# Slot attention and a GELU feed-forward: a longer pinned order, with forty copies on another engine

## The chip, the cores and the metric

One core of a Trainium2 chip. A core has five engines that each work through a list of instructions of their own, strictly in its order: TensorE (PE in the profile, matrix products, PEld its weight loads), VectorE (DVE), ScalarE (ACT), GpSimd (POOL) and SyncE (SP, which here issues the transfers between HBM and the on-chip memory). They wait for each other through semaphores. The metric is the time of one execution in microseconds (us), as the median of several.

## The reference

```python
def _attn_ref(q, k, v, phi):                      # batch 8, heads 8, seq 576, head_dim 64, 32 slots
    a = np.exp(phi - np.max(phi, axis=2, keepdims=True))      # softmax over the sequence
    a = a / (np.sum(a, axis=2, keepdims=True) + 1e-09)
    k_m = np.einsum('bhsm,bhsd->bhmd', a, k)
    v_m = np.einsum('bhsm,bhsd->bhmd', a, v)
    scores = np.matmul(q, k_m.transpose(0, 1, 3, 2)) / np.sqrt(q.shape[-1])
    attn = np.exp(scores - np.max(scores, axis=-1, keepdims=True))
    attn = attn / (np.sum(attn, axis=-1, keepdims=True) + 1e-09)
    return np.matmul(attn, v_m)

def _moe_ref(x, w_in, w_out):                     # x (4608, 512), w_in (512, 2048), w_out (2048, 512)
    h = x @ w_in
    return 0.5 * h * (1.0 + erf(h / np.sqrt(2.0))) @ w_out
```

The attention's output, heads side by side, is the `x` of the second function. All arrays arrive as float32 (the two weights as float64 bit patterns in pairs of 32-bit words, which the kernel turns into float32 itself).

## The kernel before

**Stages.** Each of the 8 batches goes through the same steps. `phi` is loaded with slots on partitions (128 x 576, two groups of heads g = 0, 1), gets its maximum (`amax`, DVE, L392) and exponential (`aexp`, ACT, L398), is transposed on PE (`at`, L423) and copied out of PSUM (`atc`, L210). `slots` (PE, L531, L506) sums it against k and v, `km` scales the sums, `slotsT` and `kT` transpose and copy them. The scores follow (`n_score` for batch 0, L615; `score` for the others, L598), then a softmax over 32 slots (`max`, `sub`, `exp`, `sum`, `inv`, `mul`) whose result p is split into a high and a low part (`ph`, `pl`; for batch 0 `n_hi`, L689, and `n_lo`, L693). The value sums are not multiplied with p. They are multiplied with `w_in` first: `Up` (PE, L598) makes U = v_m @ w_in for 128 to 512 columns of the hidden layer, split by `Uh` (a copy) and `Ul` (DVE, L814). Then `h` (PE, L855) makes the hidden layer from U and p in six products per 288 rows and 128 hidden columns; `gelu` (ACT), `gh` (a copy, the high part) and `gl` (DVE, L882) prepare it, and `p` (PE, L895, line `acc`) adds twelve products with `w_out` to four accumulators. `o` copies these out. For batches 2 to 7 `p`, `o` are called `P`, `O` and work by halves.

**Weights.** `w_in` and `w_out` come in 16 slabs f each (`Lwi.f`, `Lwo.f`). Every half slab is turned into float32 by `dB` (two ACT instructions, L272 and L273), `dC`, `dS`, `dG` (DVE, L277, L285, L281) and one sum on POOL (`dDi` for w_in, `dDo` for w_out, L305); w_out is also split by `dE` (a copy) and `dF` (DVE, L311). All of this lies in the first 150 us.

**What sets the order.** A string `START` names these steps one by one, with batch, slab and half (`aexp.0.1` is batch 0, group 1; `gelu.0.3.1` is batch 0, hidden slab 3, second half of the rows; `dB.0.1` is slab 0 of w_out, `dB.0.0` that of w_in). The program issues them in this order, so each engine's list is the string cut down to that engine's steps, and a dependency ties every instruction to the one before on its engine. A letter behind a colon (`:a`, `:d`) gives a copy to ACT or DVE. Behind the string a plan with due times (`put`, `prepare`, `columns`, `run`) does what is left. Before, the string ends with `p.1.15`, the last product of batch 1. `W.k.i` are matmuls on ones whose result nobody reads.

**Buffers.** A second string, `HOME`, gives each slab, each key and value tile and each output a place in memory by name (`raw_3:U0` reuses the place of `raw_0`). A load into a used place waits on SP until the earlier user is through, and all loads behind it wait too. In PSUM the tiles of `Up`, `score`, `slots`, `slotsT` and of batch 1's `at` share one place (`ps_at`, one buffer), so each waits until the one before is copied out.

Of the kernel before, what the change touches and what calls it, by code (L numbers as in the profile page):

```python
# [62 lines left out]
Ul.0.3 score.1.0 dC.4.0 dS.4.0 Lwi.6 gelu.0.2.0 h.0.3.0 Lwo.7 gh.0.2:a dF.3 dB.5.0
gelu.0.3.0 h.0.3.1 dDi.4 dB.6.0 sT.1.0.1 Lwo.5 dB.5.1 sT.1.0.0 Lwi.8 Up.0.4.1 p.0.1
dC.5.0 dS.5.0 dG.5.0 Uh.0.4:d Ul.0.4 h.0.4.0 gelu.0.3.1 gh.0.3:a max.1.0 dG.6.0 Lq.1.1
dDi.5 Up.0.5.1 h.0.4.1 sub.1.0 exp.1.0 gl.0.2 dC.6.0 gl.0.3 dG.5.1 dC.5.1 dS.5.1 sum.1.0
gelu.0.4.1 p.0.2 Uh.0.5:d Ul.0.5 inv.1.0 dDo.5 dE.5 mul.1.0 dS.6.0 score.1.1 pT.1.0
Lwo.6 dB.6.1 Lwo.8 sT.1.1.0 p.0.3 sT.1.1.1 gelu.0.4.0 Lwi.7 gh.0.4:a dF.5 dB.7.1 gl.0.4
# [1156 lines left out]
```

## Time and profile before

| | |
|---|---|
| median of 3 runs | 703.35 us (702.97 to 704.49) |
| profiled execution | 704.61 us, of which the span from first to last instruction is 702.8 us |
| PE | busy 691.1 us of the span |
| DVE, ACT, POOL | busy 388.6, 298.4 and 46.6 us |
| moved | 64.37 MB, mean 92 GB/s |

The span is what the trace shows; 1.8 us of the profiled execution lie around it. PE is on the chain that ended last for 94% of the span. A busy PE is not a PE at full clock: its granted clock is at one of two levels, and the lower one doubles most of its durations.

### The profile page before, as it was taken

The numbers are of one execution on the slowest core, as the hardware profiler recorded it, in microseconds if no ns is written. First come the engines' busy times: TensorE is split into PE (matmuls) and PEld (weight loads), VectorE is DVE, ScalarE is ACT, GpSimd is POOL, SyncE is SP. The second block draws the span as 40 slices with busy tenths as digits, with TensorE's granted clock in tenths as the row PEclk, the third lists the DMA queues.
The fourth block names the chain that finished last, engine by engine and source line by source line (L and its number), as shares of the span: only waits on it lengthen the run. The fifth ranks groups of instructions, "written<-read, shape, count | busy, mean of one in ns | idle before, by whom it ended". The sixth has DMA issues, their size and how long they took to land.

```text
span 702.8 us, 12357 instructions
## 1 busy us (share of the span) xinstructions
PE 691.1 (98%) x4940; PEld 576.6 (82%) x4940; DVE 388.6 (55%) x705; ACT 298.4 (42%) x768; POOL 46.6 (7%) x39
## 2 busy tenths in 40 slices
PE   7999999999999999999999999999999999999997
PEld 5767787887878888888887888888877888888886
DVE  4989998954755366534943346433834346432222
ACT  4588766862615264524553224222531225322220
POOL 1232243310000000000000000000000000000000
PEclk7599999999999999999999999999999999999999
DMA  8954451416253571145600200020000200000001
GB/s 318 329 211 172 154 197 62 133 29 212 86 142 117 177 217 23 65 137 159 190 1 32 82 2 31 1 98 1 30 1 31 83 1 31 1 31 0 31 1 45
DMA packets 30716, 64.37 MB, mean 92 GB/s; under 512 B 3780, under 2 KB 8644, under 8 KB 30660
## 3 DMA queue, kind: packets, MB, share of 16 engines
q1 hardware_dynamic: 30564, 63.46, 27.6%
q8 instruction: 39, 0.64, 0.4%
q10 hardware_dynamic: 96, 0.13, 0.1%
q14 instruction: 17, 0.14, 0.1%
HBM read 54.13 MB, written 9.44 MB: 90 GB/s over the span
## 4 chain that ended last, share of the span: by engine, by line
PE 94%; DMA 1%; DVE 1%; SPq 0%; ACT 0%; issue 0%
PE acc L895 50%; PE h L855 29%; PE tacc L895 6%; PE pu L598 4%; PE psc L598 1%; PE psc L506 1%; DMA raw<-w_in 1%; PE pk L531 1%; PE x L506 1%; SPq L345 0%; PE pk L506 0%; PE psc L519 0%; PE psc L560 0%; DVE aT L210 0%; PE x L519 0%
## 5 line engine op out<-in xcount | busy, mean ns | idle before, releaser
L855 PE MATMUL h<-p_hi,U 128*128 128x288 f32 x1024 | 203.8, 298 | 0.0
L895 PE MATMUL acc<-wo_hi,gh 128*128 128x512 f32 x512 | 200.6, 392 | 0.0
L895 PE MATMUL acc<-wo_hi,gl 128*128 128x512 f32 x512 | 199.7, 390 | 0.0
L895 PE MATMUL acc<-wo_lo,gh 128*128 128x512 f32 x512 | 199.6, 390 | 0.0
L867 ACT ACTIVATE gf<-h 128x256 f32<-128x256 f32 x192 | 74.0, 387 | 265.0 <-issue 206.4
L855 PEld LDWEIGHTS h<-p_hi,U 128*128 128x128 f32 x1024 | 164.0, 188 | 23.0 <-issue 8.3
L210 DVE CAST gh<-gf 128x512 fp32r<-128x512 f32 x109 | 46.9, 430 | 167.4 <-ACT gf L867 165.3
L895 PEld LDWEIGHTS acc<-wo_hi,gh 128*128 128x128 f32 x512 | 96.5, 188 | 21.1 <-DVE gl L882 3.4
L895 PEld LDWEIGHTS acc<-wo_hi,gl 128*128 128x128 f32 x512 | 96.1, 188 | 21.5 <-DVE gl L882 0.9
L895 PEld LDWEIGHTS acc<-wo_lo,gh 128*128 128x128 f32 x512 | 96.1, 188 | 15.8
L855 PE MATMUL h<-p_lo,U 128*128 128x288 f32 x512 | 108.8, 294 | 0.1
L882 DVE TENSOR_TENSOR gl<-gf,gh 128x512 fp32r<-128x512 f32 x128 | 94.3, 736 | 15.2 <-ACT gh L210 5.7
L855 PEld LDWEIGHTS h<-p_lo,U 128*128 128x128 f32 x512 | 81.4, 188 | 0.6 <-DVE p_lo L693 0.6
L814 DVE TENSOR_TENSOR U<-pu,U 128x512 fp32r<-128x512 f32 (+2 forms) x50 | 40.8, 834 | 42.0 <-ACT U L210 41.8
L869 ACT ACTIVATE tails<-h 128x32 f32<-128x32 f32 x192 | 37.4, 195 | 0.0
L598 PE MATMUL pu<-w_in_sb,kT 64*32 64x512 f32 (+2 forms) x624 | 34.4, 528 | 0.4 <-ACT kT L210 0.4
L210 ACT CAST U<-pu 128x512 fp32r<-128x512 f32 (+2 forms) x42 | 30.4, 759 | 7.4 <-PE pu L598 7.3
L305 POOL TENSOR_TENSOR w_in_sb<-y,raw 128x512 int32<-128x512 int32 x16 | 23.8, 1493 | 43.8 <-DVE y L285 11.8
L305 POOL TENSOR_TENSOR y<-y,raw 128x512 int32<-128x512 int32 x16 | 21.9, 1374 | 56.5 <-DVE y L285 23.9
L272 ACT ACTIVATE y<-raw 128x512 f32<-128x512 f32 x32 | 21.6, 675 | 8.9 <-issue 4.3
L895 PE MATMUL tacc<-wo_hi,gh_t 128*128 128x512 f32 x64 | 25.0, 391 | 0.0
L895 PE MATMUL tacc<-wo_hi,gl_t 128*128 128x512 f32 x64 | 24.9, 389 | 0.0
(119 smaller groups left out, 581.5 us busy)
## 6 DMA issues: line engine op xcount, KB each, us to landing
kv<-kv SPq DMA_DIRECT2D x48, 256.0 KB, 6.5
raw<-w_out SPq DMA_DIRECT2D x16, 512.0 KB, 5.6
raw<-w_in SPq DMA_DIRECT2D x16, 512.0 KB, 4.5
out<-o SPq DMA_DIRECT2D x16, 512.0 KB, 2.7
q<-qT SPq DMA_DIRECT2D x9, 576.0 KB, 8.8
phi<-phiT SPq DMA_DIRECT2D x16, 288.0 KB, 4.5
aT<-phiN SPq DMA_DIRECT2D x6, 512.0 KB, 4.7
q<-qT SPq DMA_DIRECT2D x10, 288.0 KB
```

The source lines that it names most:

```text
L210: return e.copy(dst, src) if e is nc.scalar else e.tensor_copy(dst, src)
L272: nc.scalar.activation(y, high.bitcast(F32), AF.Abs, scale=2.0**16)
L305: nc.gpsimd.tensor_tensor(w, y, low, op=ALU.add)
L506: nc.tensor.matmul(pk[32 * j : 32 * j + 32, : 2 * D], st["aT", b][:, c, g, 32 * j : 32 * j + 32], st["kv", b, g, c][:, :, j, :], start=(c ...
L531: nc.tensor.matmul(pk[32 * j : 32 * j + 32, w0 * D : (w0 + n) * D], st["aT", b][:rows, c, g, 32 * j : 32 * j + 32], t[:rows, w0 : w0 + n, ...
L598: nc.tensor.matmul(ps[g][M * j : M * j + M], st["kT", b][rows, t, M * j : M * j + M], moving[j][rows], start=True, stop=True,)
L814: nc.vector.tensor_sub(u[:, ..., 1, :], pu, u[:, ..., 0, :].bitcast(F32))
L855: i = nc.tensor.matmul(h[:, :HS], u[g][w], x[:, g, :], start=(n == 0), stop=(n == 3 * G - 1))
L867: nc.scalar.activation(gf[:, f % 2 * n : f % 2 * n + n], h[:, :n], AF.Gelu)
L869: nc.scalar.activation(t, h[:, n:HS], AF.Gelu)
L882: nc.vector.tensor_tensor(g_of("gl", *k), g_of("gf", *k), g_of("gh", *k).bitcast(F32), op=ALU.subtract)
L895: nc.tensor.matmul(acc, x, w[:, f, :], start=(first and n == 0), stop=(last and n == 2))
```

## The change

`START` is replaced: 694 steps become 850, and it now ends within batch 2 (its first half of rows is done, the second begun, scores of batch 3 and slot sums of batch 4 among it). Of the steps in both strings 40 run on another engine: 29 copies go from DVE to ACT (8 `Uh`, 8 `gh`, 5 `atc`, 4 `o`, 2 `dE`, 2 `ph`), 11 from ACT to DVE (4 `gh`, 4 `dE`, 2 `Uh`, 1 `atc`); with those in the rest of the program DVE's list has 22 copies fewer and ACT's 22 more. Nothing else changes engine, and no instruction of PE is added or taken away: 4,125 matmuls of the same shapes stand in both lists. The new string `PLACES` allots each place in memory once, ahead of all use, since the order of first use is another one now; it takes the place of `first_tiles`. `anat` is issued as its two halves `aadd` and `ax`. The store of an output of batches 0 and 1 becomes a step of its own, `os`. Line numbers shift by 13 to 20.

```diff
+PLACES = """
+kT:1024*3 phi:4608*1 nm:8*2 sm:8*2 aT:5120*1 rz:8*2 mx:72*2 smx:72*2 U0:8192*1 U4:8192*1
...
+"""
 START = """
-W.4.3 Lphi.0.0 amax.0.0 aexp.0.0 at.0.0.0 Lphi.0.1 amax.0.1 aexp.0.1 anorm.0 atc.0.0.0:d
-at.0.1.0 atc.0.1.0 at.0.0.4 Lwo.0 at.0.1.4 atc.0.1.4:d Lkv0.0.0 Lkv0.1.0 atc.0.0.4:d
...
+Lphi.0.0 Lphi.0.1 Lwo.0 Lkv0.0.0 Lkv0.1.0 amax.0.0 Lq.0.0 amax.0.1 aexp.0.0 Lwi.0 Lwo.1
+at.0.0.0 Lq.0.1 dB.0.1 dC.0.1 aexp.0.1 dS.0.1 dG.0.1 atc.0.0.0:a at.0.1.0 anorm.0 W.4.3 dDo.0
...
-    def first_tiles():
-
-        for tag in ("mx", "smx"):
-            sb.tile([P, G * SB], F32, tag=tag, name=f"{tag}_first")
+    for x in PLACES.split():
+        tag, size, n = x.replace("*", ":").split(":")
+        sb.tile([P, int(size) // 4], F32, tag=tag, name=f"place_{tag}", bufs=int(n))
...
-        if f == NF - 1 and j % 2:
-            r = b * S + (j - 1) * P
-            nc.sync.dma_start(
-                out[r : r + 2 * P, :].rearrange("(c p) n -> p c n", p=P), st["o", b, j // 2]
-            )
+
+    def store(b, j):
+        r = b * S + (j - 1) * P
+        nc.sync.dma_start(
+            out[r : r + 2 * P, :].rearrange("(c p) n -> p c n", p=P), st["o", b, j // 2]
+        )
...
-        put(tn + 1, f"anat.{b}", *(f"aexp.{b}.{g}" for g in range(G)), f"anorm.{b}")
+        put(tn + 1, f"aadd.{b}", f"ax.{b}", *(f"aexp.{b}.{g}" for g in range(G)), f"anorm.{b}")
```

The first place: ACT's list from its first exponential on, before (`phi_0`, `sm_0` are the exponential of batch 0, `y_0`, `raw_0` the conversion of slab 0, `pt_0_g_c` a transposed piece of group g):

```order
L398 ACTIVATE phi_0_101,sm_0_105<-phi_0_101,nm_0_103 128x576 x2
L210 COPY aT_0_107<-pt_0_1_0_120 128x4x128
L272 ACTIVATE y_0_171<-raw_0_130 128x512
L273 ACTIVATE raw_0_130<-raw_0_130 128x512
L549 ACTIVATE km_0_201<-pk_0_0_144,rz_0_117 128x64
L549 ACTIVATE km_0_201<-pk_0_1_180,rz_0_117 128x64
```

and now:

```order
L415 ACTIVATE phi_0_136,sm_0_154<-phi_0_136,nm_0_149 128x576
L289 ACTIVATE y_0_167<-raw_0_139 128x512
L290 ACTIVATE raw_0_139<-raw_0_139 128x512
L415 ACTIVATE phi_0_136,sm_0_154<-phi_0_136,nm_0_149 128x576
L229 COPY aT_0_159<-pt_0_0_0_160 128x4x128
L229 COPY aT_0_159<-pt_0_1_0_175 128x4x128
L229 COPY aT_0_159<-pt_0_0_4_191 64x128
L562 ACTIVATE km_0_217<-pk_0_0_194,rz_0_181 128x64
L229 COPY aT_0_159<-pt_0_1_4_189 64x128
L229 CAST wo_hi_79<-y_0_167 128x512
L562 ACTIVATE km_0_217<-pk_0_1_223,rz_0_181 128x64
```

The conversion of slab 0, which needs the transfer of w_out, now stands between the two exponentials, and the three other `atc` copies have come over from DVE.

The second place: DVE's list from the first score maximum of batch 0 on (`mx_0_0`), before:

```order
L634 TENSOR_REDUCE mx_0_0_229<-psc_0_0_220 128x16
L639 TENSOR_TENSOR s_0_0_231<-psc_0_0_220,mx_0_0_229 128x512
L277 TENSOR_SCALAR y_1_205<-y_1_205 128x512
L285 TENSOR_SCALAR y_1_205<-y_1_205 128x512
L281 TENSOR_SCALAR raw_1_165<-raw_1_165 128x512
L649 TENSOR_REDUCE smx_0_0_249<-s_0_0_231 128x16
L653 TENSOR_SCALAR smx_0_0_249<-smx_0_0_249 128x16
L654 RECIPROCAL smx_0_0_249<-smx_0_0_249 128x16
L277 TENSOR_SCALAR y_0_171<-y_0_171 128x512
L285 TENSOR_SCALAR y_0_171<-y_0_171 128x512
L281 TENSOR_SCALAR raw_0_130<-raw_0_130 128x512
L634 TENSOR_REDUCE mx_0_1_283<-psc_0_1_237 128x16
```

and now, from shortly ahead of it:

```order
L328 TENSOR_TENSOR wo_lo_80<-y_0_167,wo_hi_79 128x512
L294 TENSOR_SCALAR y_0_167<-y_0_167 128x512
L302 TENSOR_SCALAR y_0_167<-y_0_167 128x512
L298 TENSOR_SCALAR raw_0_139<-raw_0_139 128x512
L294 TENSOR_SCALAR y_1_270<-y_1_270 128x512
L298 TENSOR_SCALAR raw_1_157<-raw_1_157 128x512
L302 TENSOR_SCALAR y_1_270<-y_1_270 128x512
L647 TENSOR_REDUCE mx_0_0_288<-psc_0_0_257 128x16
L652 TENSOR_TENSOR s_0_0_291<-psc_0_0_257,mx_0_0_288 128x512
L409 TENSOR_REDUCE nm_1_294<-phi_1_215 128x1
L662 TENSOR_REDUCE smx_0_0_299<-s_0_0_291 128x16
```

The three steps on slab 0 of w_in (`y_0`, `raw_0`) stand ahead of the first maximum now, where they stood behind it.

The third place: PE's list around the first `h`, before:

```order
L423 MATMUL pt_1_0_397<-ident_76,phi_1_311 128x128 x8
L855 MATMUL h_0_0_0_415<-p_hi_0_0_403,U_0_0_339 128x288 x2
L855 MATMUL h_0_0_0_415<-p_lo_0_0_404,U_0_0_339 128x288 x2
L423 MATMUL pt_1_4_426<-ident_76,phi_1_311 64x128 x2
L674 MATMUL pT_0_2_451<-ident_76,s_0_2_390 128x128 x2
L531 MATMUL pk_1_0_460<-kv_1_0_0_340,aT_1_396 32x128 x4
```

and now:

```order
L440 MATMUL pt_1_0_444<-ident_76,phi_1_215 128x128 x8
L687 MATMUL pT_0_0_401<-ident_76,s_0_1_369 128x128
L687 MATMUL pT_0_1_403<-ident_76,s_0_1_369 128x128
L440 MATMUL pt_1_4_470<-ident_76,phi_1_215 64x128 x2
L687 MATMUL pT_0_2_477<-ident_76,s_0_2_415 128x128 x2
L544 MATMUL pk_1_0_489<-kv_1_0_0_304,aT_1_443 32x128 x4
L544 MATMUL pk_1_0_489<-kv_1_0_4_378,aT_1_443 32x128 x4
L868 MATMUL h_0_0_0_521<-p_hi_0_0_485,U_0_0_398 128x288 x2
```

The first `h` has gone behind the slot sums of batch 1 (`pk_1_0`). Further on, `p.0.0` stands ahead of `h.0.2.0`, `h.0.2.1` and `Up.0.3.1`, behind which it stood.

## Rows read from the trace of the kernel before

**Rows 1.** The page: busy time of each engine, and the chain that ended last.

```profile
PE 691.1 (98%) x4940; PEld 576.6 (82%) x4940; DVE 388.6 (55%) x705; ACT 298.4 (42%) x768; POOL 46.6 (7%) x39
PE 94%; DMA 1%; DVE 1%; SPq 0%; ACT 0%; issue 0%
```

**Rows 2.** All waits of PE: who waited for whom, us in total, times, longest.

```profile
PE pk L531 <- DMA kv<-kv: 3.0, 2, 2.4
...
PE tn L560 <- ACT km L549: 0.6, 1, 0.6
```

**Rows 3.** Stretches: length, busy us (instructions) by engine, granted clock share, DMA share, GB/s.

```profile
10.22:34.11 23.89, 21.35 (x243) 17.63 (x232) 18.66 (x41) 11.15 (x26) 6.85 (x5) 0.50 0.96 350
34.11:37.53 3.42, 2.02 (x13) 1.03 (x11) 3.32 (x10) 2.72 (x8) 1.31 (x1) 1.00 0.35 140
37.53:40.94 3.41, 3.41 (x44) 2.55 (x45) 1.70 (x8) 2.65 (x6) 1.29 (x1) 0.50 0.34 118
40.94:250.00 209.06, 209.06 (x1592) 169.57 (x1594) 151.73 (x264) 123.77 (x265) 36.18 (x25) 1.00 0.44 142
```

**Rows 4.** ACT in order of time: start, us, line, tiles, [idle before, releaser].

```profile
4.37 0.78 ACT L398 ACTIVATE phi<-phi,nm 128x576 f32<-128x576 f32 x1 [2.14 <-DVE nm L392]
...
5.38 0.78 ACT L398 ACTIVATE phi<-phi,nm 128x576 f32<-128x576 f32 x1
...
8.05 0.66 ACT L272 ACTIVATE y<-raw 128x512 f32<-128x512 f32 x1 [0.25 <-DMA raw<-w_out]
8.61 0.66 ACT L273 ACTIVATE raw<-raw 128x512 int32<-128x512 uint32 x1
```

**Rows 5.** PE in order of time, the first 48 us, same columns.

```profile
9.83 0.78 PE L531 MATMUL pk<-kv,aT 128*32 128x64 f32 x32 [2.43 <-DMA kv<-kv]
...
12.96 0.79 PE L295 MATMUL warm<-one 128*128 128x128 f32 x2
...
15.07 7.06 PE L615 MATMUL psc<-k_blocks,q 128*128 128x64 f32 x32 [0.72 <-ACT k_blocks L210]
...
33.57 0.76 PE L855 MATMUL h<-p_hi,U 128*128 128x288 f32 x2
...
36.86 0.30 PE L423 MATMUL pt<-ident,phi 128*64 128x128 f32 x1 [1.12 <-DVE aT L210]
...
37.51 2.52 PE L531 MATMUL pk<-kv,aT 128*32 128x128 f32 x40
39.96 0.85 PE L855 MATMUL h<-p_hi,U 128*128 128x288 f32 x2
...
43.59 1.43 PE L531 MATMUL pk<-kv,aT 128*32 128x128 f32 x40
...
47.33 0.50 PE L895 MATMUL acc<-wo_hi,gh 128*128 128x512 f32 x1
```

**Rows 6.** DVE in order of time, 18 to 41 us, same columns.

```profile
18.75 0.69 DVE L634 TENSOR_REDUCE mx<-psc 128x16 f32<-128x512 f32 x1 [0.67 <-PE psc L615]
...
39.43 0.95 DVE L693 TENSOR_TENSOR p_lo<-pT,p_hi 128x64 fp32r<-128x64 f32 x4 [1.12 <-ACT p_hi L689]
```

**Rows 7.** Groups by line and shape: count, busy us, mean ns of one, idle before.

```profile
L210 DVE CAST gh<-gf 128x512 fp32r<-128x512 f32 x109 | 46.9, 430 | 167.4 <-ACT gf L867 165.3 <-ACT wo_hi L210 1.3 <-ACT gf L873 0.8
L210 ACT CAST gh<-gf 128x512 fp32r<-128x512 f32 x19 | 11.8, 622 | 4.1 <-PE acc L895 4.0
L210 DVE COPY aT<-pt 128x512 f32<-128x512 f32 x2 | 1.4, 676 | 0.0
L210 DVE CAST U<-pu 128x256 fp32r<-128x256 f32 x5 | 2.1, 421 | 0.0
L277 DVE TENSOR_SCALAR y<-y 128x512 f32<-128x512 f32 x32 | 14.9, 468 | 4.4 <-ACT y L272 4.3
```

**Rows 8.** Stretches as in rows 3, by DVE's load.

```profile
18.75:40.38 21.63, 19.16 (x207) 14.84 (x207) 19.85 (x49) 12.54 (x29) 6.89 (x5) 0.58 0.75 265
40.38:80.00 39.62, 39.62 (x374) 29.78 (x374) 37.95 (x75) 32.55 (x67) 13.12 (x9) 0.99 0.46 167
```

More of the change, by code (lines that the diff above doesn't have):

```diff
@@ L63 @@
[L63 to L68, printed above, removed]
@@ new lines @@
+Lwi.5 dG.3.1 Lwo.5 Up.0.2.1 Lphi.2.1 dS.3.1 h.0.0.1 gelu.0.0.0 dC.3.0 Lq.1.0 dDo.3 Uh.0.2:a
+dE.2:a h.0.1.0 Ul.0.2 amax.2.0 gelu.0.0.1 dF.2 slots.1.1 gelu.0.1.0 gh.0.0:a dS.3.0 dG.3.0
+h.0.1.1 gl.0.0 km.1.1 dDi.3 dE.3 slotsT.1 gelu.0.1.1 Lwo.7 dB.4.1 p.0.0 kT.1:d Lwo.6 Lwi.6
+dB.4.0 dG.4.1 dC.4.1 gh.0.1:a dF.3 h.0.2.0 dC.4.0 dS.4.1 dS.4.0 Up.0.3.1 gelu.0.2.0 dDo.4
+dB.5.1 h.0.2.1 Uh.0.3:d Ul.0.3 h.0.3.0 gl.0.1 gelu.0.2.1 dB.5.0 dG.5.1 score.1.0 p.0.1
+gh.0.2:a sT.1.0.0 Lq.1.1 dG.4.0 gelu.0.3.0 Lwi.7 dE.4 dC.5.0 dDi.4 amax.2.1 sT.1.0.1 dC.5.1
@@ new lines @@
+Lwo.8 h.0.3.1 dF.4 mw.2 gl.0.2 Up.0.4.1 gelu.0.3.1 dS.5.0 p.0.2 dG.5.0 gh.0.3:d dDi.5 aexp.2.0
+max.1.0 Uh.0.4:a dB.6.0 Ul.0.4 sub.1.0 h.0.4.0 gl.0.3 exp.1.0 h.0.4.1 dS.5.1 dG.6.0 dDo.5
+Up.0.5.1 sum.1.0 p.0.3 Uh.0.5:a inv.1.0 dC.6.0 mr.2 Ul.0.5 gelu.0.4.1 mul.1.0 Lwi.8 gelu.0.4.0
+dE.5 dS.6.0 pT.1.0 gh.0.4:a score.1.1 dDi.6 dB.6.1 h.0.5.0 sT.1.1.1 sT.1.1.0 h.0.5.1 dF.5
+ph.1.0:a gl.0.4 dB.7.0 Up.0.6.1 dC.6.1 p.0.4 max.1.1 gelu.0.5.0 Uh.0.6 dC.7.0 gelu.0.5.1
+Ul.0.6 gh.0.5:a sub.1.1 pl.1.0 Up.1.0.4 gl.0.5 exp.1.1 dG.7.0 h.0.6.0 dS.7.0 Uh.1.0 dDi.7
@@ L111 @@
+gl.2.0.6 gelu.2.14.0 aadd.4 pl.2.1 h.2.15.0 h.2.0.1 gelu.2.15.0 h.2.1.1 P.2.0.6 ax.4
+gh.2.0.7:a gl.2.0.7 P.2.0.7 gelu.2.1.1 score.3.1 score.3.0 sT.3.1.0 slots.4.0 sT.3.0.1
+slots.4.1 O.2.0.0:a Lphin.5 Lkv.5.0.1 Lkv.5.1.3 aexp.4.1 Lkv.5.0.3 Lkv.5.1.2 Lkv.5.1.0
+Lkv.5.0.4 gelu.2.0.1 Lkv.5.1.1 O.2.0.1 aexp.4.0 gh.2.1.0:a gl.2.1.0 anorm.4 km.4.1 sT.3.0.0
+Lphi.5.0 sT.3.1.1 km.4.0 Lkv.5.0.0 Lkv.5.0.2 Lphi.5.1
 """
@@ L954, in evict @@
                 ("o", b, j // 2),
-                lambda: sb.tile([P, 2, DM], F32, **home(f"o_{b}_{j}")),
+                lambda: sb.tile([P, 2, DM], F32, **home(f"o_{b}_{j // 2 * 2}")),
             )
@@ L1000, in slot_attention_gelu_ffn @@
     }
+    st.update({("far", "pu", b, f): 1 for b in range(3, B) for f in (4, 12)})
+    st.update({("far", "psc", b, 1): 1 for b in range(3, B)})
+    st.update({k: 1 for k in (("far", "xt", 3), ("far", "pu", 2, 12))})
     done = set()
@@ L1044, in slot_attention_gelu_ffn @@
     put(t + 13, "slotsT.2", "kT.2")
-    st.update({("far", "pu", b, f): 1 for b in range(3, B) for f in (4, 12)})
-    st.update({("far", "psc", b, 1): 1 for b in range(3, B)})
-    st.update({k: 1 for k in (("far", "xt", 3), ("far", "pu", 2, 12))})
     for hf, at in ((0, n + 22), (1, n + 26)):
@@ L1167, in slot_attention_gelu_ffn @@
             if end:
-                behind += [f"o.{b}.{j}.{f}" for j in range(NT)]
+                for j in range(NT):
+                    behind += [f"o.{b}.{j}.{f}"]
+                    if f == NF - 1 and j % 2:
+                        behind += [f"os.{b}.{j}"]
         else:
```

130 lines of the change are left out of this document (65 added, 65 removed).

## Prediction

> **What bounds the kernel now.** I read the page first, then the waits of PE, then stretches of equal clock, then the first 48 us row by row. PE is busy for 691.1 of 702.8 us and is 94% of the chain that ended last [rows 1]. So only PE's idle time and PE's slow time can be won. Both lie in one place. From 40.94 us on PE has no idle time at all (209.06 of 209.06 us up to 250 us) and runs at its upper level, 2.4 GHz [rows 3]; the waits of PE, the longest 2.4 us for keys and values, all lie before [rows 2]. Between 10.22 and 34.11 us it is granted 0.50 of its clock, the lower level of 1.2 GHz, as again between 37.53 and 40.94 us, with 1.00 between [rows 3]. The first product with w_out starts at 47.33 us [rows 5]. In the start DVE is the partner: from the first score maximum at 18.75 us until the last low part of p at 40.38 us (39.43 plus 0.95) it is busy for 19.85 of 21.63 us [rows 6, 8], and in the next 40 us for 37.95 of 39.62 us [rows 8]. All the same PE never waits there.
>
> PE's 4,125 matmuls are the same before and after. **So the change can gain in the first 41 us alone**, and behind them it can only keep or lose. The lengthened part of the string, within batches 1 and 2, has nothing to gain: PE is already full there. I therefore walk through the start, engine by engine in the new order, with the durations of these rows, up to the point where both orders have done the same work on PE: the end of `p.0.0`, `h.0.2.0`, `h.0.2.1` and `Up.0.3.1`.
>
> **Step 1, up to the first scores: 2.7 us later.** Before, the second exponential follows the first at 5.38 us [rows 4]. Now the conversion of slab 0 of w_out stands between them, and it starts at 8.05 us, when its transfer lands; its two instructions reach to about 9.15 us, where the next can start (8.61 plus about 0.55, the step from the first to the second) [rows 4]. The transfers ahead of it on SP are the same five, so I take the same landing. The second exponential then ends about 10.0 us instead of 6.2. Behind it on PE come four transposes (0.85 us at the lower level, by the 0.21 us of one matmul of the 32 in 7.06 us [rows 5]), now two pairs of warming matmuls (0.85 us; a pair is 0.79 us long at most [rows 5]), two short transposes (0.4), and on ACT the copy that the slot sums need (0.3). They start at 12.8 us instead of 9.83 [rows 5]. From there to the first score matmul 5.24 us passed (15.07 less 9.83), with one warming pair in the way at 12.96 us that now stands later [rows 5]; I take 5.0. The scores start at 17.8 us instead of 15.07: plus 2.7.
>
> **Step 2, from the scores to batch 1's slot sums: 2.7 us won back.** Before, this takes 22.44 us (37.51 less 15.07 [rows 5]) with DVE full. What DVE does between the first maximum and the last low part is 19.85 us [rows 8]. Of this, two high parts of U and one large transposed copy go to ACT (2 x 0.42 and 0.68, together 1.5 us [rows 7]); three conversion steps of slab 0 go ahead of the maximum, where DVE now waits anyway (about 0.35 and 0.35 in a row and 0.55, together 1.3; one alone reads 0.47 [rows 7]); two of slab 3 go behind (0.9); one step of the split of w_out slab 1 and small copies come in (0.8). That leaves 16.9 us. The first maximum is at 21.45 us (18.75 plus 2.7). With some 1.6 us in which DVE must wait for PE's second scores, for U's high part on ACT and for the high part of p, the last low part is ready at 39.95 us instead of 40.38. ACT, busy for 12.54 of the 21.63 us [rows 8], hides the three copies; without that cover they would cost 0.38 to 0.62 us each, by the dearest row of a copy there [rows 7]. PE's transposes of batch 1 wait for the second low part of U at 33.8 us, and its slot sums start at 37.55 us, against 37.51 [rows 5]. The loads for them land well ahead, as I read SP's list: the two that wait for the place of earlier keys are issued at about 38 us in both orders.
>
> **Step 3, to equal work: minus 0.7 or plus 0.9 us.** What is missing by then is the first `h`, which before ran from 33.57 us in PE's free time [rows 5]. Now it lies on the path: 0.85 us at the upper level (0.85 us is the first pair and its entry at 39.96 us; six in a row take 0.8 to 1.0). Against this stands the clock. Before, a stretch without a gap of transposes and the first `h` was followed by the upper level at 34.11 us, then an idle 1.12 us by the fall at 37.53 us [rows 3, 5]. In the new order the transposes of batch 1, of p and the slot sums follow each other from 33.9 us with 0.3 us of gaps. If the clock has risen when the slot sums start, they take 1.43 us as those at 43.59 us, not 2.52 [rows 5], and the next `h` takes 0.9 instead of 1.4: 1.6 us won, 0.85 and 0.04 paid, minus 0.7. If it rises at 40.94 us as before, plus 0.9. `p.0.0` starts at 44.4 or 46.0 us. It needs its low part from DVE, which has 3.75 us of other steps ahead of it and delivers it at about 44.5 to 45.2 us; so nothing more is won by a faster PE here, and DVE is late next.
>
> The Trainium skill (TensorE: Matmul & The Clock Gate, What's actually happening) states that the gate runs freely and does not restart with the kernel, so that the point of the rise moves from run to run. By that the same order could give either of the two results above; one profile cannot show it.
>
> **Step 4, behind 47 us: nothing, or a loss.** The remaining 22 copies less on DVE (0.38 to 0.68 us each [rows 7]) relieve an engine that is 96% busy up to 80 us [rows 8] but keeps nobody waiting. ACT has 7.1 us free there [rows 8]. I take zero; the bounds are zero and, if two new waits appear of the size of the smaller ones of before (0.6 us [rows 2]), plus 1.2.
>
> **Sum.** The span becomes 702.8 - 0.7 = 702.1 us or 702.8 + 0.9 = 703.7 us. The profiled execution is 704.61 us, 1.26 us above the median of 703.35; I carry the difference over to the median: 702.65 or 704.25 us.
>
> **The rivals.**
> *A, the clock returns early* (forecast): 702.65 us, 36%. For it speaks that the new order keeps PE denser between 34 and 41 us.
> *B, the clock returns at 40.94 us as before*: 704.25 us, 21%. The slot sums of batch 1 were inside a slow stretch before, too.
> *C, slower*: the clock is still low when PE is full. In the new order PE has a gap before batch 1's transposes (31.9 to 33.8 us, waiting for DVE). If the gap and the dependence on DVE go on until the slot sums, the lower level lasts beyond 40.94 us. For a further slow stretch as long as that of 37.53 to 40.94 us, 3.41 us [rows 3], full work at half the rate costs 1.7 us: 704.25 + 1.7 = 705.95 us, 16%. It decides if the second low part of U is done later than about 35 us.
> *D, faster*: the w_out transfer lands before the first exponential is through (about 5.2 us). Then the conversion costs only its own 1.15 us and step 1 shrinks by 2.7 us, which DVE passes on: 2.5 us less than A, 700.15 us. The row speaks against it (8.05 us [rows 4]), but it is one landing of one execution; together with all that my walk gives DVE too much work for, 18%. The Trainium skill (DMA: Bandwidth & Descriptors, Specifications) gives 358 GB/s from HBM and 0.6 us to the first byte; an estimate by it puts the landing of the first 1.1 MB at about 4.5 us, which would be this rival; the trace has 8.05 us, and the trace decides.
> *E, new waits behind 47 us*: A to B plus 1.2, about 705.0 us, 9%.
> That the change does nothing it says is A to B as well: beyond the start it moves work between engines that PE does not wait for.
>
> **How the numbers follow.** About 0.2%, 1.4 us, is what a measurement can tell from no change: faster is under 701.95, slower over 704.75 us. I give each case a spread of 1 us. Faster: D nearly whole and a quarter of A, 28%. Slower: C nearly whole, most of E, a quarter of B, 28%. Between: 44%. The range for 8 in 10 goes from D to a little above C, 700.2 to 706.2 us; A alone would be 701.6 to 703.7 us.
>
> **What would show it.** Step 1: in the new profile ACT's second exponential starts about 9.2 us, the scores at 17.8 us. Step 2: the slot sums of batch 1 at 37.5 us, DVE with some 1.6 us of gaps before the last low part of p. Step 3: the stretch of granted clock around them, 1.00 from 37.5 us (A), from 40.9 (B) or later (C); the first product with w_out at 44 to 46 us. Step 4: PE busy without a gap from then to 250 us. The forecast is wrong in its core if the scores start before 16 us, if PE idles over 1 us behind 47 us, or if the clock falls there.

## The result and the profile after

The changed kernel takes **712.07 us** (median; 709.53 to 712.5) beside 703.83 us of the kernel before (702.97 to 704.59): a ratio of 1.0111, 95% interval 1.0099 to 1.0123. It is slower by 1.1%. Its profiled execution took 710.29 us with a span of 708.5 us, 5.7 us more than the 702.8 us of before.

The page of the changed kernel (busy time, chain that ended last), against [rows 1]:

```profile
PE 692.1 (98%) x4940; PEld 577.0 (81%) x4940; DVE 370.6 (52%) x683; ACT 307.4 (43%) x790; POOL 45.2 (6%) x39
PE 95%; DMA 2%; ACT 2%; DVE 0%; issue 0%; SPq 0%
```

Both engines moved as the diff says: DVE 18 us less, ACT 9 us more. That tells nothing of the time. The waits of PE do, against [rows 2] (who waited for whom, us in total, times, longest):

```profile
PE h L868 <- ACT tails L882: 3.7, 1, 3.7
PE pt L440 <- ACT phi L415: 2.8, 2, 2.1
PE acc L908 <- ACT gh L229: 1.4, 1, 1.4
PE pt L440 <- DVE U L827: 1.3, 1, 1.3
```

The first and the third line have no counterpart in [rows 2]. Where they lie, the stretches of equal granted clock show, against [rows 3] (columns as there):

```profile
13.04:16.46 3.42, 2.54 (x39) 2.13 (x29) 1.53 (x4) 2.78 (x7) 0.00 (x0) 1.00 1.03 420
16.46:33.52 17.06, 14.84 (x161) 12.03 (x160) 15.33 (x39) 13.23 (x29) 5.43 (x4) 0.50 1.03 383
33.52:60.00 26.48, 26.03 (x273) 20.25 (x271) 23.56 (x51) 21.11 (x48) 9.71 (x7) 1.00 0.71 237
60.00:250.00 190.00, 189.98 (x1389) 155.02 (x1392) 120.38 (x213) 103.70 (x231) 27.81 (x20) 1.00 0.39 122
250.00:255.39 5.39, 2.67 (x70) 2.03 (x62) 0.48 (x1) 3.57 (x5) 0.00 (x0) 1.00 0.42 117
255.39:265.63 10.24, 7.90 (x22) 6.35 (x23) 5.87 (x13) 8.83 (x16) 0.00 (x0) 0.50 0.92 323
265.63:300.00 34.37, 34.37 (x228) 28.94 (x235) 20.76 (x39) 18.11 (x48) 0.00 (x0) 1.00 0.11 22
```

Three things are to be seen. The start has its upper clock level from 33.52 us, where before it had it for good from 40.94 us [rows 3]. From 60 to 250 us nothing is lost: 189.98 of 190 us busy at 1.00. And between 250 and 265.63 us, where the kernel before was full at 1.00, PE idles and its clock then falls to 0.50 for 10.24 us.

The start, against [rows 4] (ACT) and [rows 5] (PE), in order of time:

```profile
6.56 0.66 ACT L289 ACTIVATE y<-raw 128x512 f32<-128x512 f32 x1 [1.26 <-DMA raw<-w_out]
...
7.68 0.76 ACT L415 ACTIVATE phi<-phi,nm 128x576 f32<-128x576 f32 x1
```

```profile
14.95 5.69 PE L628 MATMUL psc<-k_blocks,q 128*128 128x64 f32 x32 [0.44 <-issue]
...
34.34 1.43 PE L544 MATMUL pk<-kv,aT 128*32 128x128 f32 x40 [0.45 <-ACT aT L229]
...
41.44 0.47 PE L908 MATMUL acc<-wo_hi,gh 128*128 128x512 f32 x1
...
46.17 0.69 PE L868 MATMUL h<-p_hi,U 128*128 128x288 f32 x4
```

Equal work is reached in the middle of that last row, at 46.4 us, where before `p.0.0` was through at 50.3 us: **the start wins 3.9 us** in this execution. So behind it 9.6 us are lost (5.7 plus 3.9). The median of the changed kernel lies 1.8 us above this execution and 8.2 us above the kernel before; if the loss behind is the same each time, the start wins some 1.4 us at the median (an estimate: 9.6 less 8.2). PE and ACT there, at the end of the string:

```profile
247.90 0.39 PE L908 MATMUL acc<-wo_hi,gl 128*128 128x512 f32 x1
248.22 1.20 PE L611 MATMUL psc<-q,kT 64*32 64x288 f32 x32
249.35 1.95 PE L519 MATMUL psc<-kv,aT 128*32 128x128 f32 x64
251.24 0.45 PE L532 MATMUL psc<-kvw,aT 64*32 64x128 f32 x16
...
252.24 0.43 PE L868 MATMUL h<-p_hi,U 128*128 128x288 f32 x2
256.37 0.85 PE L868 MATMUL h<-p_hi,U 128*128 128x288 f32 x2 [3.71 <-ACT tails L882]
...
259.54 0.79 PE L908 MATMUL acc<-wo_hi,gh 128*128 128x512 f32 x1 [1.36 <-ACT gh L229]
```

```profile
246.31 0.19 ACT L882 ACTIVATE tails<-h 128x32 f32<-128x32 f32 x1
251.79 0.59 ACT L229 COPY o<-acc 128x512 f32<-128x512 f32 x1 [5.30 <-PE psc L532]
252.39 1.28 ACT L415 ACT_TABLE_LOAD   x1
253.68 0.77 ACT L415 ACTIVATE phi<-phi,nm 128x576 f32<-128x576 f32 x1
...
254.56 1.28 ACT L880 ACT_TABLE_LOAD   x1
255.85 0.38 ACT L880 ACTIVATE gf<-h 128x256 f32<-128x256 f32 x1
...
256.82 1.28 ACT L415 ACT_TABLE_LOAD   x1
...
258.89 0.60 ACT L229 CAST gh<-gf 128x512 fp32r<-128x512 f32 x1
```

The first half of batch 2 ends with the product at 247.90 us (through at 248.29). ACT has nothing to do from 246.50 to 251.79 us. Then come the output copy (`O.2.0.0`), an exponential of batch 4 between two table loads, and only at 255.85 us the GELU `gelu.2.0.1`, whose `h` PE had made before 243 us. There are two PSUM places for `h`; this GELU frees one, so PE's fourth `h` of the second half (`h.2.3.1`) waits 3.71 us for it. Then the other exponential, again with its load, stands ahead of `gh.2.1.0`: 1.36 us. The two waits are 5.1 us; the 7.90 busy us at half clock cost 3.95 us more; together 9.0 of the 9.6 us (the 3.95 us are an estimate: half of the 7.90).

### The profile page after: what moved, and what is told of

Its sections match the earlier page's. It is cut to its first block, busy times and chain, and to the rows that moved or that the text cites. A ratio compares the mean times of both kernels' runs of the same rounds, so it can differ in the third digit from the quotient of the medians.

```text
span 708.5 us, 12352 instructions
## 1 busy us (share of the span) xinstructions
PE 692.1 (98%) x4940; PEld 577.0 (81%) x4940; DVE 370.6 (52%) x683; ACT 307.4 (43%) x790; POOL 45.2 (6%) x39
## 4 chain that ended last, share of the span: by engine, by line
PE 95%; DMA 2%; ACT 2%; DVE 0%; issue 0%; SPq 0%
PE acc L908 50%; PE h L868 29%; PE tacc L908 6%; PE pu L611 5%; DMA kv<-kv 1%; PE psc L611 1%; PE psc L519 1%; DMA raw<-w_out 1%; PE pk L544 1%; PE pt L440 1%; PE x L519 1%; ACT L415 0%; ACT phi L415 0%; PE psc L628 0%; PE pk L519 0%
## 5 line engine op out<-in xcount | busy, mean ns | idle before, releaser
L229 DVE CAST gh<-gf 128x512 fp32r<-128x512 f32 x98 | 41.4, 423 | 169.4 <-ACT gf L880 159.2
L895 DVE TENSOR_TENSOR gl<-gf,gh 128x512 fp32r<-128x512 f32 x128 | 88.9, 696 | 44.9 <-ACT gh L229 36.0
L298 DVE TENSOR_SCALAR raw<-raw 128x512 uint16<-128x512 uint16 x32 | 24.8, 784 | 1.0 <-ACT raw L290 1.0
L908 PE MATMUL tacc<-wo_lo,gh_t 128*128 128x512 f32 x64 | 24.9, 389 | 0.0
```

What stands on the lines that cost most here:

```text
L229: return e.copy(dst, src) if e is nc.scalar else e.tensor_copy(dst, src)
L298: nc.vector.tensor_single_scalar(low, high, 0x8000, op=ALU.bitwise_and)
L895: nc.vector.tensor_tensor(g_of("gl", *k), g_of("gf", *k), g_of("gh", *k).bitcast(F32), op=ALU.subtract)
L908: nc.tensor.matmul(acc, x, w[:, f, :], start=(first and n == 0), stop=(last and n == 2))
```

## The experiments

All are the changed kernel with its string edited; a diff shows steps of the string. Times are medians, ratios are to the kernel before on the same chip, with 95% interval; "span" is that of the profiled execution. The first theory was that the exponentials with their table loads are the cause at the end, and that the start's 3.9 us are a gain to be kept.

**cut_tail: end the string at `P.2.0.7`.**

```diff
 ... gl.2.0.7 P.2.0.7
-gelu.2.1.1 score.3.1 score.3.0 sT.3.1.0 slots.4.0 sT.3.0.1 slots.4.1 O.2.0.0:a ... Lphi.5.1
```

> The changed kernel with its pinned string ended at P.2.0.7; the last steps of the string (second half of batch 2, slot sums and exponentials of batch 4, scores of batch 3) are left to the plan again. Theory (the start gains some 4 us, the whole loss of some 9.5 us sits in the last twenty steps of the string): 699 to 700.5 us, that is 3.5 to 4.5 us under the kernel before; PE has no wait over 0.5 us between 245 and 270 us and its granted clock stays at 1.00 there. Rival (the loss comes from the longer pinning as such, the place where string and plan meet): the wait of about 5 us moves to the new end, and the time stays at 708 or more. Rival (the clock would fall near 255 us in any case): 704, with the granted clock at 0.50 for some 10 us and no wait ahead of it.

Measured: 705.91 us, ratio 1.0015 (0.9999 to 1.0030), span 706.4 us. Better than the changed kernel by 6 us, but not the 699 to 700.5 us expected. The wait for the GELU is gone. Another came, for an output copy (`O.2.0.0`, which the plan leaves on DVE, as in the kernel before):

```profile
258.62 0.80 PE L903 MATMUL acc<-wo_hi,gh 128*128 128x512 f32 x1 [2.10 <-DVE o L224]
```

So it is not the last steps of the string as such: the plan, taking over there, is late as well. Here too the output copy on ACT started only when the slot sums were through (254.88 us, idle for 3.43 us until PE's `psc<-kvw`).

**exp_behind: the exponentials moved behind `gh.2.1.0`.**

```diff
-... aexp.4.1 ... gelu.2.0.1 ... O.2.0.1 aexp.4.0 gh.2.1.0:a gl.2.1.0 anorm.4
+... gelu.2.0.1 ... O.2.0.1 gh.2.1.0:a aexp.4.1 aexp.4.0 anorm.4 gl.2.1.0
```

> The changed kernel with its full string, but the two exponentials of batch 4 (aexp.4.1, aexp.4.0) and anorm.4 stand behind gh.2.1.0 instead of around gelu.2.0.1. Theory (the exponentials with their table loads, 1.28 us each, hold up the gelu that frees the hidden layer's PSUM place): the wait of PE at 252.7 us falls from 3.7 us to under 2 us (what is left is the output copy O.2.0.0, which waits for PE's last product, and one gelu), the second wait of 1.4 us goes, the granted clock does not fall, and the time is 699 to 702 us. Rival (the output copy ahead of the gelu is the cause, the exponentials only lie beside it): the waits stay at 3 us or more and the time at 706 to 710 us.

Measured: 708.39 us, 1.0051 (1.0037 to 1.0066). The time is in the rival's range, but PE's wait for the GELU is gone, as the theory had it. The edit had a fault of its own: `anorm.4`, a DVE step that needs the exponentials, stood ahead of `gl.2.1.0`, and PE waited for that:

```profile
PE acc L906 <- DVE gl L893: 3.2, 1, 3.2
```

A new wait of nearly the old size took the place of the first; the question stayed open.

**cut_oldstart and cut_oldletters: the start of the kernel before on the base of cut_tail.**

```diff
-Lphi.0.0 ... p.0.0                    (changed order, changed engines)
+W.4.3 Lphi.0.0 ... (same steps)       cut_oldstart: order and engines of before
+... atc.0.0.0:d ... dE.0:d Uh.0.0:d   cut_oldletters: changed order, engines of before
```

> As the run cut_tail, but the steps up to p.0.0 stand in the order of the kernel before, with its engines; from there to P.2.0.7 the changed string. Theory (the first 46 us alone bring the gain): 703 to 704.5 us, as the kernel before, first product with w_out at about 47 us. Rival (the part from 46 to 250 us brings some of it): 700 to 702 us. Rival (the start gains nothing and its lead is a matter of when the clock rose in one execution): the same time as cut_tail within 0.5 us.

> As the run cut_tail, but the copies of the start whose engine differs (atc of batches 0 and 1, dE.0, dE.1, Uh.0.0, Uh.0.1) are back on the engines of the kernel before; the order is the changed one. If the relief of DVE makes the gain of the start: 702.5 to 704 us, with DVE later than in cut_tail at the scores of batch 0 and the slot sums of batch 1. If the order makes it: within 0.7 us of cut_tail.

Measured: 715.35 us, 1.0164 (1.0149 to 1.0180), and 705.99 us, 1.0034 (1.0021 to 1.0047). The first fell outside all three expectations: up to `p.0.0` it was as quick (first product at 44.12 us, in cut_tail at 44.51), but from 47.9 us PE waited for a copy that was late on DVE. Ahead of that copy DVE stood idle for 7.29 us until phi of batch 2 landed: the edit puts its loads directly ahead of the maximum that reads it, since the old start doesn't contain them (PE's wait, then DVE):

```profile
PE pu L606 <- DVE kT L224: 3.9, 1, 3.9
```

```profile
50.61 0.75 DVE L404 TENSOR_REDUCE nm<-phi 128x1 f32<-128x576 f32 x1 [7.29 <-DMA phi<-phiT]
51.28 0.41 DVE L224 COPY kT<-tn 128x256 f32<-128x256 f32 x1
```

This start and this rest don't fit together as they are; the run judges neither. The second could not be told from cut_tail (the intervals overlap), with the loss at 256 us in both; it is taken up again below.

**o_early, o_early_exp: the output copies ahead of the scores of batch 3**, then also the exponentials behind `gl.2.1.0`.

```diff
-gelu.2.1.1 score.3.1 ... slots.4.1 O.2.0.0:a ... O.2.0.1
+gelu.2.1.1 O.2.0.0:a O.2.0.1 score.3.1 ... slots.4.1 ...
```

> The changed kernel with its full string; only the two output copies of batch 2's first half (O.2.0.0, O.2.0.1) stand ahead of the scores of batch 3 instead of behind the slot sums of batch 4. Theory (a step waits for everything that PE was given ahead of it in the string; in the changed kernel the copy therefore starts at 251.8 us, 3.5 us after its sums were complete at 248.3): the copy starts within 0.6 us of the last product of the first half, the exponentials' two table loads lie in time in which ACT was idle, PE's first wait falls from 3.7 to under 1.5 us, and the second one, for gh.2.1.0 behind the other exponential, stays at 1 to 2 us; 704 to 709 us. Rival (the place of the copy is of no account, the exponentials alone hold the gelu up): the first wait stays at 3 us or more, 709 to 712 us.

> As o_early, and the two exponentials of batch 4 stand behind gl.2.1.0 (their reciprocal, anorm.4, behind them). Theory (copy and exponentials together are the whole of the end's loss): no wait of PE over 0.5 us between 240 and 270 us, the granted clock stays at 1.00 there, and the time is 699 to 702.5 us, under the kernel before by what the start gains (0.8 us when w_out lands at 8.1 us, 3.6 us when it lands at 6.6 us and the clock is up early). Rival (the place where string and plan meet costs in itself): a wait of 2 us or more shows up elsewhere between 250 and 300 us, 704 us or more.

Measured: 711.49 us, 1.0114 (1.0099 to 1.0129), and 706.97 us, 1.0056 (1.0041 to 1.0070). The theory of o_early fell, and o_early_exp missed its 699 to 702.5 us. The time of o_early is in its rival's range, but the order was not put to the test, for the copy had not moved: though it now stands ahead of the slot sums in the program, the copy began only when they were through (two copies in one row, o_early):

```profile
252.55 1.07 ACT L227 COPY o<-acc 128x512 f32<-128x512 f32 x2 [5.29 <-PE psc L530]
```

The row names the slot sums' last matmuls, `psc<-kvw`, and the string of places, the same in both kernels, says why: `kvw_4:wy1 ... o_2_0:wy1`. The output is written over the last keys and values of batch 4, so it must wait until the slot sums of batch 4 have read them. The kernel before has the same reuse. There the slot sums stood two slabs of products ahead of the half's end, and the copy was released by its own sums:

```profile
255.41 0.59 ACT L210 COPY o<-acc 128x512 f32<-128x512 f32 x1 [2.25 <-PE acc L895]
```

**place: the two places exchanged; place_exp: with the exponentials behind as well.**

```diff
-kvw_5:wy0 ... o_2_0:wy1 ... o_2_1:wy1
+kvw_5:wy1 ... o_2_0:wy0 ... o_2_1:wy0
-P.2.0.3 Lkv.5.1.4 h.2.8.0 ... slots.4.1 O.2.0.0:a
+P.2.0.3 h.2.8.0 ... slots.4.1 Lkv.5.1.4 O.2.0.0:a
```

> The changed kernel with its full order, but the outputs of batch 2 take the place wy0 and the last keys and values of batch 5 (kvw_5) the place wy1, where it was the other way round; the load of kvw_5 (Lkv.5.1.4) stands behind slots.4.1. In the changed kernel the output copy O.2.0.0 writes over kvw_4, which the slot sums of batch 4 read last, at 251.7 us. Theory (this reuse, not the order on ACT, dates the copy): the copy starts at once behind the last product (248.3 us in the changed kernel's own time) instead of 251.8; with table load, exponential and table load behind it the gelu that PE waits for comes at 252.4 instead of 255.9, so PE's first wait falls from 3.7 to under 0.8 us; the second one, for gh.2.1.0 behind the other exponential, grows to about 2 us; 704 to 709 us. Rival (the copy waits for everything PE was given before it, wherever it writes): it starts at 251.8 us again, and the time is that of the changed kernel, 709 to 712 us.

> As place, and the two exponentials of batch 4 stand behind gl.2.1.0, O.2.0.1 directly behind O.2.0.0. Theory: copy at 248.3 us, gelu.2.0.1 and gh.2.1.0 through by 250.6, before PE has ended its slot sums; no wait of PE for them; the exponentials (1.28 + 1.9 + 1.28 us) then hold up the next gelu, gelu.2.2.1, until about 257, for a wait of 0 to 1.5 us; 700 to 705 us.

Measured: 705.77 us, 1.0028 (1.0016 to 1.0041), and 706.65 us, 1.0036 (1.0020 to 1.0052). The place alone brings 6.3 of the 8.2 us, with the order on ACT as it was. In place the copy waits 0.46 us, for its own sums, ahead of the scores, which start at 250.80 us:

```profile
249.55 0.59 ACT L227 COPY o<-acc 128x512 f32<-128x512 f32 x1 [0.46 <-PE acc L906]
```

PE's 3.7 us are gone; for `gh.2.1.0` behind the second exponential it waits 1.3 us, where 2 were expected. **This settles what dated the copy:** in the program it still stands behind the slot sums. place_exp took the wait for `gh.2.1.0` away as well and came to the same time, since another of 2.6 us began at 269.6 us, behind a DVE idle for 4.99 us until phi of batch 5 landed; the next pair takes that up.

**gelu_early: the GELU, its high and low part and the exponentials put into ACT's idle 5.3 us, places as they were. gelu_early_phi: also the loads of phi of batch 5 ahead of those of its keys and values.**

```diff
-gelu.2.1.1 score.3.1 ... slots.4.1 O.2.0.0:a ... Lkv.5.0.2 Lphi.5.1
+gelu.2.1.1 gelu.2.0.1 gh.2.1.0:a gl.2.1.0 aexp.4.1 aexp.4.0 anorm.4
+Lphi.5.0 Lphi.5.1                     gelu_early_phi alone
+score.3.1 ... slots.4.1 O.2.0.0:a O.2.0.1 ...
```

> The changed kernel with its places as they are, but gelu.2.0.1, gh.2.1.0, gl.2.1.0 and then the two exponentials of batch 4 stand directly behind gelu.2.1.1, in the 5.3 us in which ACT has nothing to do, ahead of the two output copies. Theory (all of the end's loss is the order of eight ACT steps around one late copy): no wait of PE over 0.3 us between 240 and 270 us, the granted clock stays at 1.00 there, and the time is what is left of the start's gain: 700 to 703 us. Rival (the remaining waits of the other variants come from the plan behind the string): a wait of 1 us or more stays between 255 and 265 us, 704 to 707 us.

> As gelu_early, and the two loads of phi of batch 5 stand directly behind the exponentials of batch 4, ahead of the ten loads of keys and values of batch 5. In gelu_early they left at 259.9 and 262.4 us, behind those; the maximum of batch 5 (amax.5.0) held DVE for 4.9 us until the first had landed at 265.4, gh behind it came late, and PE waited 2.4 us for it. Theory (that is all that is left of the loss behind 47 us): DVE does not wait for phi, PE waits nowhere over 0.5 us behind 35 us, the granted clock stays up, and the time is 699.5 to 702.5 us, under the kernel before by the gain of the start. Rival (another step of the string's end is late behind it): a new wait of 1 us or more between 255 and 300 us, 703.5 us or more. Rival (the start gains nothing on average): no wait behind 35 us, and yet 703 to 704.5 us.

Measured: 706.6 us, 1.0036 (1.0022 to 1.0050), and 703.34 us, 0.9996 (0.9979 to 1.0012). In gelu_early no wait over 0.3 us is left between 240 and 262 us, but DVE and then PE wait further on (gelu_early, DVE, then PE):

```profile
265.40 0.75 DVE L407 TENSOR_REDUCE nm<-phi 128x1 f32<-128x576 f32 x1 [4.88 <-DMA phi<-phiT]
...
270.05 0.38 DVE L227 CAST gh<-gf 128x512 fp32r<-128x512 f32 x1
```

```profile
270.48 0.50 PE L906 MATMUL acc<-wo_hi,gh 128*128 128x512 f32 x1 [2.43 <-DVE gh L227]
```

The string puts the loads of phi behind the loads of keys and values on SP's queue; the kernel before issued them at 247.5 us, gelu_early at 259.9. The maximum that needs phi heads DVE's list, and everything behind it waits 4.88 us. In the changed kernel itself this didn't show, since PE and DVE were late already. The time of gelu_early_phi, 703.34 us, misses the theory's 699.5 to 702.5; no wait over 0.3 us is left behind 35 us, so it is the case of the last rival, a start that gains nothing on average. With the loads moved up, DVE's wait is gone (gelu_early_phi, stretches):

```profile
60.00:240.00 180.00, 179.98 (x1290) 146.72 (x1289) 117.26 (x212) 100.15 (x226) 28.71 (x21) 1.00 0.40 130
240.00:300.00 60.00, 59.72 (x465) 49.30 (x465) 35.05 (x65) 35.92 (x83) 0.00 (x0) 1.00 0.28 88
```

**cut_p6 and cut_batch1: end the string elsewhere**, ahead of `P.2.0.6`, so that the plan puts scores and slot sums where the kernel before has them; or at `p.1.15`, where its string ends.

```diff
 ... h.2.0.1 gelu.2.15.0 h.2.1.1
-P.2.0.6 ax.4 ... Lphi.5.1             cut_p6
 ... tg.1.0 gelu.2.0.0 p.1.15
-o.1.0.15 o.1.1.15 ... Lphi.5.1        cut_batch1
```

> The changed string ended ahead of P.2.0.6, so that the plan puts the scores of batch 3 and the slot sums of batch 4 where the kernel before has them, ahead of the last products of batch 2's first half, and with them the exponentials, the output copies and the load of phi of batch 5. Theory (the loss is the order of the string's last thirty steps and nothing else): no wait of PE over 0.5 us behind 35 us, 699.5 to 702.5 us, within 0.7 us of gelu_early_phi. Rival (a meeting of string and plan costs wherever it lies, as 8.3 us with the cut at p.1.15 and 2.1 us with the cut at P.2.0.7): a wait of 1 us or more between 240 and 290 us, 703.5 us or more.

> The changed string ended at p.1.15, where the string of the kernel before ends; the plan does all of batch 2. Theory (the plan places the output copies and exponentials right, so no end loss): PE waits nowhere over 0.5 us behind 60 us, 700 to 703.5 us, within 0.5 us of o_early_exp. Rival (the pinned first half of batch 2 brings something of its own): 1 us or more over o_early_exp. Rival (a meeting of string and plan costs wherever it lies): a wait of 2 us or more between 205 and 240 us.

Measured: cut_p6 **701.7 us, 0.9980 (0.9966 to 0.9994)**, cut_batch1 713.34 us, 1.0154 (1.0131 to 1.0177). cut_p6 beats both kernels, by little. It was to lie within 0.7 us of gelu_early_phi and is 1.6 us under it; their intervals overlap, and why they differ is open. Behind 60 us nothing is lost in it up to 300 us:

```profile
60.00:240.00 180.00, 179.98 (x1306) 146.68 (x1305) 120.18 (x214) 101.01 (x225) 29.68 (x21) 1.00 0.41 130
240.00:300.00 60.00, 60.00 (x464) 49.36 (x463) 36.87 (x68) 31.51 (x78) 0.00 (x0) 1.00 0.30 88
```

In cut_batch1 string and plan meet badly: four output sums of batch 1, left out of the string, come behind a whole softmax of batch 2 on DVE, and PE waits 8.3 us for the place of its accumulator (DVE, then PE):

```profile
204.83 2.48 DVE L955 TENSOR_TENSOR o<-acc,part 128x512 f32<-128x512 f32 x4
```

```profile
205.57 0.79 PE L891 MATMUL tacc<-wo_hi,gh_t 128*128 128x512 f32 x1 [8.30 <-DVE o L955]
```

So the rival of a costly meeting holds at p.1.15 and at P.2.0.7, and not at P.2.0.6: what decides is what the string has left undone where it ends.

**What the start gains.** With the end free of waits, the start can be measured alone. cut_p6_oldletters puts its copies back (nine to DVE, one to ACT), and four kernels put `aexp.0.1` ahead of `dB.0.1`.

```diff
-... atc.0.0.0:a ... dE.0:a ... Uh.0.0:a   cut_p6_oldletters
+... atc.0.0.0:d ... dE.0:d ... Uh.0.0:d
-... dB.0.1 dC.0.1 aexp.0.1 ...            cut_p6, gelu_early_phi, gelu_early, o_early_exp, each with _first
+... aexp.0.1 dB.0.1 dC.0.1 ...
```

> As cut_p6, with the copies up to p.0.0 whose engine differs back on the engines of the kernel before, the order unchanged. On the base of cut_tail this came to the same (705.99 beside 705.91), but with another loss at 256 us in both. If the copies that went to ACT bring the start's gain: a ratio of 1.000 to 1.002, DVE later at the scores. If the order brings it: 0.997 to 0.999, as cut_p6.

> As cut_p6 (the changed string ended ahead of P.2.0.6), and the second exponential of batch 0 ahead of the conversion of slab 0 of w_out. If the wait of step 1 is the start's remaining cost (PE waited 2.6 to 3.3 us for that exponential in gelu_early_phi and cut_p6, 0.7 with it in front): a ratio to the kernel before of 0.995 to 0.9965, that is 1 to 2 us under cut_p6's 0.998. If keys and values and DVE then take its place: 0.9975 to 0.9985, as gelu_early_phi_first with 0.9982.

> As gelu_early_phi, and the second exponential of batch 0 ahead of the conversion of slab 0 of w_out. Theory of step 1 (the start of the changed kernel pays for w_out's landing): 0.5 to 2 us under gelu_early_phi. Rival (the time won there is lost to DVE or to keys and values before 60 us, as gelu_early_first beside gelu_early has it): equal or up to 2 us over gelu_early_phi.

> As o_early_exp, and the second exponential of batch 0 (aexp.0.1) stands ahead of the conversion of slab 0 of w_out (dB.0.1) again. Theory (in the changed order all of the start waits for w_out's landing, by 2.1 to 3.4 us in the runs so far): PE's wait of 2.1 to 3.4 us for the second exponential falls under 1 us, the slot sums of batch 0 then wait for keys and values instead (they landed at 8.7 to 9.8 us), and the time is 0.5 to 2 us under o_early_exp. Rival (what the start gives back there is lost again to DVE, since the steps of slab 0 are late): the same as o_early_exp within 0.4 us.

> As gelu_early, and the second exponential of batch 0 ahead of the conversion of slab 0 of w_out (as in o_early_exp_first, where PE's wait for it was 0.8 us instead of 1.5 to 4.3). Theory: 0.5 to 2 us under gelu_early and 2 to 4 us under the kernel before: 699 to 702 us. Rival (what the start gains is taken back before 60 us): the same as gelu_early within 0.4 us.

Measured: cut_p6_oldletters 704.38 us, 1.0015 (1.0002 to 1.0028). The interval doesn't touch that of cut_p6, nor that of cut_p6_first, which ran on the same chip beside it (0.9967 to 0.9998): **the copies moved to ACT are worth some 0.35%, 2.5 us**, and the changed order without them is no faster than before. On the base of cut_tail the same edit showed 0.2%, with intervals that overlap. The traces show 0.9 us of it. From the scores to the slot sums of batch 1 cut_oldletters takes 21.45 us and cut_tail 20.58 (37.42 less 16.84), with the scores at 7.06 us in both (cut_oldletters):

```profile
16.12 7.06 PE L623 MATMUL psc<-k_blocks,q 128*128 128x64 f32 x32 [0.30 <-issue]
...
37.57 1.43 PE L539 MATMUL pk<-kv,aT 128*32 128x128 f32 x40 [0.78 <-DVE aT L224]
```

PE waits there for DVE, and in cut_p6_oldletters as well: 1.8 us for the low part of U, where cut_p6 has 1.3, and 0.9 us for transposed copies, where cut_p6 waits 0.5 us for ACT (cut_p6_oldletters, waits):

```profile
PE pt L434 <- DVE U L821: 1.8, 1, 1.8
...
PE pt L434 <- DVE aT L223: 0.5, 1, 0.5
...
PE pk L538 <- DVE aT L223: 0.4, 1, 0.4
```

Where the other 1.6 us lie is not shown.

cut_p6_first took 701.64 us, 0.9983 (0.9967 to 0.9998); gelu_early_phi_first 702.49 us, 0.9982 (0.9968 to 0.9996); o_early_exp_first 706.57 us, 1.0038 (1.0024 to 1.0051), beside 1.0056 for o_early_exp. gelu_early_first 708.3 us, 1.0059 (1.0045 to 1.0073), beside 1.0036. In all four the scores start at 12.96 to 13.72 us, earlier than in any run of the changed start without the exchange (14.13 to 17.00). Yet the ratio goes down twice by less than the intervals are wide, stays once and goes up once. A gain of the exchange is not shown.

## Why the prediction was wrong

The forecast was 702.65 us, in a range of 700.2 to 706.2; the time is 712.07 us. The forecast said that nothing would be lost behind 47 us; that is where it failed (step 4). All three signs that it named for being wrong in its core came: scores before 16 us (14.95), an idle PE behind 47 us (3.7 us), a fall of the clock there.

**Step 1 (scores 2.7 us later): the mechanism was right, the size not.** In all runs that have the changed order here, the second exponential waited for w_out and PE for it, by 1.1 to 4.3 us in the profiled executions (the longest of these waits in each). But the conversion started anywhere from 5.65 to 8.36 us; the 8.05 us of [rows 4] is near the late end, and the changed kernel's profile had 6.56. Where it was 8.07 us (cut_tail), the scores began at 16.84 us, not 17.8. The walk's terms up to the slot sums add to 12.4 us, not to the 12.8 it states, and the slot sums began at 12.43; from there to the scores 4.41 us passed, not 5.0. It also counts five transfers ahead of w_out on SP; the lists show two, both of phi, in both kernels. And the delay was not worth its size in time, as the exchange runs show.

**Step 2 (2.7 us won back by DVE's relief): right in kind, too large.** From scores to slot sums of batch 1 cut_tail took 20.6 us for 22.44 before: 1.9 us won, 0.9 of it by the copies, as cut_oldletters shows, and 1.0 by the order. The changed kernel took 19.4 us (34.34 less 14.95), but 1.4 us of its 3.0 came from scores that ran partly at the upper clock (5.69 us for 7.06).

**Step 3 (minus 0.7 or plus 0.9 us at equal work): minus 3.9 us in the profiled execution**, by the early landing and by a clock that was up from 33.52 us. With the late landing the forecast fits, `p.0.0` at 44.51 us in cut_tail, 44.4 forecast for case A, but by luck: step 1 was 1.0 us too slow and step 2 gave back 0.8 us too much. Rival C, the clock low for longer, was seen too: the profiled execution of cut_p6 (706.00 us, its slowest) had it low to 42 us and beyond:

```profile
34.00:42.00 8.00, 7.45 (x73) 5.31 (x73) 4.80 (x14) 4.97 (x13) 2.59 (x2) 0.50 0.69 225
```

Its first product came at 46.38 us. This execution is 4.3 us above the median of cut_p6, where C was priced at 1.7 to 3.3 us over B and A. On balance the start is worth between nothing and 0.2%: gelu_early_phi (0.9996) and cut_p6 (0.9980) both have the end repaired.

**Step 4 (behind 47 us zero, at most plus 1.2) is the step that failed:** 9.6 us. It held from 60 to 250 us, where [rows 3] end, and fails just behind, at the very end of the string. Rival E named waits there, but step 4 took their size from the waits of the kernel before [rows 2], and those belong to another order; they are no bound on an order that ends with other steps. What it left unread was in the program: ACT's list, where `gelu.2.0.1` stands behind an output copy and an exponential between two table loads; the places, where that copy reuses what the slot sums still read; SP's list, where phi comes behind eight other loads. What the runs showed in place of zero: waits of 3.71 and 1.36 us, and a clock at 0.50 behind them. Step 4 also priced a wait at its length; after 3.7 us of it the clock fell and took another 3.95 us.

Three parts were shown one by one: the reused place (place), the order on ACT (exp_behind, gelu_early), and the late phi (gelu_early_phi). PE's 3.7 us need the first two together: either repair alone takes that wait away. Nothing else is left (59.72 and 60.00 of 60 us busy in the two repaired ends). That all this sits at the string's end because what follows it didn't count in making it is likely, but was not tried. Nor was it tried by itself what it costs that the changed string puts the copy `O.2.0.0` on ACT, where the kernel before has it on DVE.

## What to carry to other kernels

Where part of an order is written out, read its last steps on every engine and queue against the first steps behind it: what they leave undone, and who waits. A step's date is set by its place in memory as well as by its data; a copy whose target another engine still reads starts no earlier by being put further up in its own engine's list (o_early). A bottleneck engine with no idle time has little to win and everything to lose, so bound the loss by what the new order makes wait, not by the waits of the old one.

## What the runs showed of the hardware

The same transfer of w_out let the conversion start between 5.65 and 8.36 us from one profiled execution to the next, over 14 executions with the same two transfers ahead of it on SP; one landing is a sample.

The granted clock can be missing from a trace. cut_tail shows 1.00 from 10 to 34 us, but its score matmuls took 7.06 us, as before at 0.50 [rows 3, 5] (a stretch of cut_tail, and PE there):

```profile
10.00:34.00 24.00, 21.42 (x255) 17.72 (x256) 15.73 (x40) 15.94 (x37) 6.71 (x5) 1.00 0.98 355
```

```profile
16.84 7.06 PE L623 MATMUL psc<-k_blocks,q 128*128 128x64 f32 x32 [0.24 <-issue]
```

The durations decide. The Trainium skill (TensorE: Matmul & The Clock Gate, Seeing it yourself) says that such records have been seen to be unreliable, and this trace agrees.

A table load cost 1.28 us and no more: in the changed kernel the exponential's last instruction ended at 254.55 us, the load ran from 254.56, the GELU started at 255.85. The Trainium skill (ScalarE: Activation LUTs, What ACT_TABLE_LOAD costs) gives 1283 ns for the load, which agrees, and about 1380 ns of drain with it, for which these rows leave no time.
